# GpSimd adds the exponentials of pair 13 and of five second halves; TensorE sums what is left in one round

## The chip, the core and the metric

The kernel runs on one core of one Trainium2 chip. The metric is the time of the program on the device in microseconds (us). Engines are named as in the profile: PE is TensorE, DVE is VectorE, ACT is ScalarE, POOL is GpSimd, and SP only issues transfers here.

## The reference

The reference is attention, a soft mixture of experts and a two-layer MLP, all in float32 with the MLP's weights in float64:

```
scores = rope(q) @ rope(k).T / 8           # 4 x 8 heads, 576 positions, 64 wide
attn   = exp(scores - rowmax); attn /= sum(attn) + 1e-9
x      = attn @ v                          # becomes 2304 tokens x 512
x      = softmoe(x, phi, w1, w2)           # 8 experts, 32 slots
out    = relu(x @ w_in)**2 @ w_out
```

The change touches only the division: how the sum of a row's exponentials is formed.

## The kernel before

The 32 heads are worked in 16 pairs, numbered 0 to 15, two heads side by side on 128 partitions. Keys stand on partitions and queries along the columns. The 576 queries of a pair are two halves of 288 (h0 and h1). The 576 keys are four full units of 128 (u0 to u3) for each half, and one unit BOTH that holds the last 64 keys of both halves, so a pair has nine score units.

For one pair the work runs like this. SP loads the transposed q and k, plain and swapped (`load`). POOL applies the rotation in six operations, three each for k (t = 0) and q (t = 1) (`rope_pair`, recorded at L543). ACT rounds the result to a high part (`parts_pair`, L577), and POOL subtracts it to get a low part (L543 too). PE forms one set of products of high parts (`max_unit`, L654), and DVE reduces them to a stand-in for the maximum of each row (L665). PE transposes these maxima (`max_rows`, L684), and SP writes them back into SBUF as a row by a DMA (L703). Then `st_unit` forms the scores of a unit on PE from three products of high and low parts (L738) and subtracts the maximum with one more (L745); ACT takes the exponential (L758) into a buffer P. `pv_unit` multiplies it with V on PE (L789, and L784 for BOTH). `norm` sums the exponentials (L813), inverts on DVE and scales, and `logits` multiplies the finished rows with phi (L863, L868) and transposes them for the experts (L886).

The sum has two parts. POOL adds the first two units of a half into `acc` (L766). PE then multiplies `acc`, the other units and BOTH with a column of ones, 32 columns of the array for each, so that four such matmuls stand side by side; a round is two things by two heads. With four things (`acc`, u2, u3, BOTH) there are two rounds. For the pairs in `LATE`, 14 and 15, POOL adds u2 and u3 to `acc` too (L771), but not u3 of pair 15's second half; there the sum has two things and one round, and that last half has three things, whose second round uses two of the four places.

The order of all this is written out by hand. The table `Plan.ORDER` holds, for each kind of operation and engine, a rank for each operation in the order in which the program creates them; `retime` makes the rank its due time, and `emit` places operations in each engine's queue, the most urgent ready one first, by a table of costs. Engines then run their queues in that order and wait on semaphores. PE's operations have modes (r for scores and maxima, c and b for V, q for sums and logits, f for transposes), since they divide the array in different ways. The raw q and k of a pair lie in one of two buffers, so the load of pair p is issued when the low parts of pair p - 2 are done. Buffers P of the late pairs, and the buffers of raw data, parts and V, are given over to expert weights (`free`, L1174) as soon as their last readers are done.

After the attention come the slots and the experts (from about 295 us), fed by weights that SP loads, and the MLP (from about 335 us, L1806).

Of the kernel before, what the change touches and what calls it, by code (L numbers as in the profile page):

```python
# [38 lines left out]
class Plan:  # L39
# [29 lines left out]
            17, 19, 55, 79, 117, 150, 194, 224, 273, 305, 346, 361, 429, 454, 526, 531, 631, 633, 721, 724, 815, 818, 910, 914, 1013, 1015, 1101, 1104, 1193,  # L69
            1196, 1261, 1268  # L70
        ),
        ("parts_pair", "POOL", None): (
            22, 28, 60, 86, 124, 160, 199, 230, 279, 314, 359, 369, 435, 460, 532, 543, 637, 648, 732, 742, 825, 836, 922, 929, 1023, 1032, 1112, 1120, 1202,
            1210, 1273, 1281
# [6 lines left out]
        ),  # L81
        ("load", "SP", None): (
            36, 99, 173, 176, 180, 237, 240, 242, 322, 323, 327, 373, 377, 379, 468, 471, 473, 557, 561, 565, 659, 662, 665, 753, 755, 758, 846, 849, 852, 942,
            946, 949, 1043, 1045, 1047, 1131, 1133, 1136
        ),
        ("windows", "ACT", None): (
            23, 30, 82, 81, 156, 132, 226, 217, 309, 296, 406, 408, 499, 502, 606, 608, 698, 701, 791, 794, 884, 887, 988, 990, 1078, 1081, 1168, 1171, 1265,
            1275, 1331, 1332
# [24 lines left out]
        ("max_rows", "SP", None): (  # L113
            51, 62, 134, 136, 219, 222, 312, 317, 415, 417, 509, 510, 615, 618, 707, 710, 800, 803, 893, 896, 997, 1000, 1087, 1090, 1177, 1180, 1270, 1274, 1358,
            1355, 1422, 1418
# [11 lines left out]
            5, 6, 7, 8, 9, 10, 80, 83, 89, 91, 95, 101, 146, 148, 152, 155, 166, 170, 249, 252, 255, 266, 270, 275, 363, 453, 552, 655, 747, 841, 935, 1036, 1125,  # L127
            1214, 1302, 1368
# [1843 lines left out]
```

## Time and profile before

| | us |
|---|---|
| median of 3 runs | 566.4 (566.14 to 568.69) |
| the profiled execution | 565.09 |
| its span | 563.3 |
| PE busy | 544.0 (97%) |
| DVE busy | 398.6 (71%) |
| ACT busy | 295.7 (52%) |
| POOL busy | 229.9 (41%) |

The share is an average over stages: POOL does nearly all of its work in the first 285 us, and the DMA engines most of theirs between 265 and 340 us. The strip of 40 slices on the profile's page shows this; one slice is 14.1 us. The granted clock of PE is 1.00 in every stretch.

### The profile page before, as it was taken

How to read it: one execution, taken by the hardware profiler on the slowest of the kernel's cores; microseconds unless marked ns; L12 is line 12 of the kernel's file. 1: busy time of each engine (PE TensorE's matmuls, PEld its weight loads, DVE VectorE, ACT ScalarE, POOL GpSimd, SP SyncE). 2: the span in 40 equal slices, each digit the busy share in tenths (PEclk: the TensorE clock that was granted, in tenths of full speed). 3: DMA queues.
4: the chain of work that ended last, by engine and by line, in shares of the span. 5: the costliest groups of instructions: out<-in, count | busy, mean ns of one | idle time of the engine just before them, and what ended most of it. 6: DMA issues, size and time to landing. Idle time of an engine off the chain costs nothing.

```text
span 563.3 us, 13271 instructions
## 1 busy us (share of the span) xinstructions
PE 544.0 (97%) x5406; PEld 416.7 (74%) x5406; DVE 398.6 (71%) x878; ACT 295.7 (52%) x568; POOL 229.9 (41%) x178
## 2 busy tenths in 40 slices
PE   4999999999999999999999999999999999999996
PEld 3656666566665666666642258999999999999996
DVE  6587788888897887876468748965775595554553
ACT  2334545664555655544426548975944564354440
POOL 4999999988889788723610000000000000000000
PEclk9999999999999999999999999999999999999999
DMA  7447796877784357222989997132200220000333
GB/s 237 139 132 184 167 249 188 221 192 195 210 219 117 93 144 201 100 99 101 338 295 396 409 401 255 39 111 76 76 1 1 76 76 2 1 1 1 113 113 112
DMA packets 37741, 85.68 MB, mean 152 GB/s; under 512 B 12176, under 2 KB 12848, under 8 KB 36528
## 3 DMA queue, kind: packets, MB, share of 16 engines
q1 hardware_dynamic: 37398, 84.24, 48.3%
q8 instruction: 42, 0.69, 0.5%
q10 hardware_dynamic: 282, 0.59, 0.4%
q14 instruction: 19, 0.16, 0.1%
HBM read 77.92 MB, written 6.82 MB: 150 GB/s over the span
## 4 chain that ended last, share of the span: by engine, by line
PE 81%; DMA 9%; DVE 5%; POOL 2%; ACT 1%; issue 1%; SPq 0%; DVEq 0%
PE bank L1806 35%; PE bank L738 11%; PE obank L789 11%; PE bank L654 5%; PE bank L813 5%; PE bank L745 3%; PE obank L1736 3%; DVE mcol L665 2%; DMA w__1345<-in_w_dram 2%; DMA tEb<-in_w_dram 2%; DMA tLb<-in_w_in_dram 2%; PE obank L784 2%; PE bank L886 2%; DMA ident<-in_ident_dram 1%; POOL arena L543 1%; DMA w__448<-in_w_dram 1%
## 5 line engine op out<-in xcount | busy, mean ns | idle before, releaser
L758 ACT ACTIVATE tO<-bank 128x576 f32<-128x576 f32 x140 | 84.2, 650 | 84.4 <-PE bank L745 83.3
L665 DVE TENSOR_REDUCE mcol<-bank 128x2 f32<-128x576 f32 x144 | 103.2, 749 | 22.6 <-PE bank L654 13.1
L543 POOL TENSOR_TENSOR arena<-arena 128x576 f32<-128x576 f32 x78 | 111.0, 1444 | 8.8 <-DMA arena<-in_qk_dram 8.0
L1806 PE MATMUL bank<-w,tEb 128*128 128x256 f32 x864 | 106.5, 279 | 0.1
L1806 PEld LDWEIGHTS bank<-w,tEb 128*128 128x128 f32 x864 | 103.5, 188 | 2.4 <-issue 1.6
L789 PE MATMUL obank<-tO,pb 128*64 128x288 f32 x496 | 74.8, 419 | 0.0
L766 POOL TENSOR_TENSOR pb<-tO 128x576 f32<-128x576 f32 x30 | 42.9, 1430 | 31.0 <-ACT tO L758 29.4
L1806 PE MATMUL bank<-w,tEa 128*128 128x256 f32 x432 | 53.0, 278 | 0.0
L1806 PEld LDWEIGHTS bank<-w,tEa 128*128 128x128 f32 x432 | 51.6, 188 | 1.2 <-issue 1.2
L1806 PE MATMUL bank<-w,tO 128*128 128x256 f32 x432 | 51.6, 277 | 0.0
L1806 PEld LDWEIGHTS bank<-w,tO 128*128 128x128 f32 x432 | 51.1, 188 | 0.0
L789 PEld LDWEIGHTS obank<-tO,pb 128*64 128x64 f32 x496 | 29.8, 136 | 22.7 <-issue 9.3
L1747 ACT ACTIVATE pb<-obank 128x384 f32<-128x384 f32 x47 | 21.7, 495 | 36.8 <-PE obank L1736 36.8
L1747 ACT ACTIVATE w__1091<-obank 128x384 f32<-128x384 f32 x48 | 21.8, 491 | 36.5 <-PE obank L1736 36.2
L654 PEld LDWEIGHTS bank<-tEb 64*128 64x128 f32 x180 | 16.3, 184 | 21.5 <-DVE mcol L665 4.4
L813 PE MATMUL bank<-tO,ones 128*32 128x288 f32 x224 | 31.9, 409 | 0.0
L654 PE MATMUL bank<-tEb 64*128 64x288 f32 x180 | 30.5, 355 | 0.7 <-DVE mcol L665 0.5
L819 DVE STREAM_TRANSPOSE bank<-bank 128x288 f32<-128x288 f32 x32 | 15.9, 496 | 19.2 <-PE bank L813 15.8
L543 POOL TENSOR_TENSOR tLb<-arena,tEb 128x576 fp32r<-128x576 f32 x20 | 28.6, 1448 | 1.3 <-ACT tEb L577 1.3
L738 PE MATMUL bank<-tEb 64*128 64x288 f32 x180 | 28.5, 313 | 0.3 <-DVE mcol L665 0.2
L1736 PE MATMUL obank<-x,tO 128*128 128x384 f32 x95 | 26.8, 336 | 0.5 <-DVE tO L1664 0.5
L738 PE MATMUL bank<-tLb,tEb 64*128 64x288 f32 x180 | 26.6, 292 | 0.0
(299 smaller groups left out, 1095.2 us busy)
## 6 DMA issues: line engine op xcount, KB each, us to landing
arena<-in_qk_dram SPq DMA_DIRECT2D x14, 576.0 KB
arena<-in_qk_dram SPq DMA_DIRECT2D x12, 512.0 KB
arena<-in_w_dram SPq DMA_DIRECT2D x8, 512.0 KB
pb<-in_v_dram SPq DMA_DIRECT2D x12, 320.0 KB
arena<-in_qk_dram SPq DMA_DIRECT2D x3, 1152.0 KB
tLb<-in_w_in_dram SPq DMA_DIRECT2D x3, 1024.0 KB
pb<-in_w_in_dram SPq DMA_DIRECT2D x3, 1024.0 KB
w__448<-in_w_dram SPq DMA_DIRECT2D x4, 512.0 KB
```

What stands on the lines that cost most here:

```text
L543: ENG[e].tensor_tensor(out=o, in0=x, in1=y, op=how)
L654: nc.tensor.matmul(on_ring(tok)[:, j, 0:HQ], lhsT=x[rows], rhs=hi[rows, 0, HALF[c]], start=(u < BOTH or c == 0), stop=(u < BOTH or c == 1),)
L665: lambda e: nc.vector.tensor_reduce(out=mcol[:, h, :, u], in_=on_ring(tok)[:, :, 0:HQ], op=ALU.max, axis=AX.X),
L738: nc.tensor.matmul(st[:, j, 0:HQ], lhsT=w[rows], rhs=q[y][rows, HALF[c]], start=(i == 0 and (u < BOTH or c == 0)), stop=False,)
L745: nc.tensor.matmul(st[:, j, 0:HQ], lhsT=pick[rows, w : w + 128], rhs=mrow[rows, HALF[c]], start=False, stop=(u < BOTH or c == 1),)
L758: lambda e: nc.scalar.activation(out=pr, in_=on_ring(tok)[:, :, 0:HQ], func=AF.Exp, scale=0.125),
L766: lambda e: nc.gpsimd.tensor_tensor(out=acc, in0=one, in1=pr, op=ALU.add),
L789: nc.tensor.matmul(BANKS[6 + h][o, 0:HQ], lhsT=vr[:, u, j, :], rhs=pr[:, j, :], start=(h == 0 and u == 0), stop=(h == 1 and u == 3))
L813: nc.tensor.matmul(sm[QUAD[2 * j + w], 0:HQ], lhsT=one, rhs=x[:, j, :], start=(i == 0), stop=(i + w + 2 > last))
L1736: lambda e, i=i, t0=t0: nc.tensor.matmul(BANKS[i][:, 0:384], lhsT=wst_of()[:, 128 * fc : 128 * fc + 128], rhs=cst_of()[:, t0 : t0 + 384], ...
L1747: lambda e, i=i, h=h: nc.scalar.activation(out=rg_of()[:, 0, h], in_=BANKS[i][:, 0:384], func=AF.Relu),
L1806: nc.tensor.matmul(BANKS[c][:, cols], lhsT=gt[:, x, 128 * c : 128 * c + 128], rhs=wo[:, fc % 2, y, cols], start=(fc % FQ == 0 and i == 0 a ...
```

## The change

`folded` now reads a table. POOL adds u2 and u3 to `acc` for the second halves of pairs 8 to 12 and for both halves of pair 13 too, besides pairs 14 and 15; that is 14 more operations at L771 (the first halves of pairs 8 to 12 stay as they were). PE's sum then has two things and one round there. In the last sum, with three things, the third is now split: its first 144 columns go to one place and its other 144 to the next, so that the second round uses all four places with half the columns. The cost that `emit` takes for a sum follows. The ranks from about pair 4 on are new for every kind of operation.

POOL's order by the new ranks, from the rope of pair 14 to pair 13's adds (rope t d is operation d of k or q; lo is a low part): rope 14 0 0, rope 14 0 1, add 10 h1 u2, lo 13 1, add 10 h1 u3, add 11 h0, lo 13 0, rope 14 0 2, rope 14 1 0, rope 14 1 1, add 11 h1, rope 14 1 2, add 11 h1 u2, rope 15 0 0, rope 15 0 1, add 11 h1 u3, rope 15 1 0, add 12 h0, rope 15 1 1, lo 14 0, rope 15 1 2, lo 14 1, rope 15 0 2, add 12 h1, lo 15 1, add 12 h1 u2, lo 15 0, add 12 h1 u3, add 13 h0 (three), add 13 h1 (three). Before: rope 14 0 0, rope 14 0 1, rope 14 1 0, lo 13 0, lo 13 1, add 11 h0, rope 14 (three), add 11 h1, rope 15 (three), lo 14 0, lo 14 1, add 12 h0, rope 15 (three), add 12 h1, lo 15 0, lo 15 1, add 13 h0, add 13 h1.

On PE the second sum of pair 12 no longer stands beside the first: between them are the first two max units of pair 15, four product units of pairs 12 and 13 and five score units of pair 13. The transpose of pair 15's maxima now follows the transposes of pair 13's `logits` instead of preceding them.

```diff
--- before
+++ after
...
         ("max_rows", "PE", "f"): (
-            46, 57, 127, 211, 302, 405, 498, 605, 697, 790, 883, 987, 1077, 1167, 1260, 1349, 1406
+            46, 57, 127, 211, 302, 405, 501, 604, 697, 791, 883, 991, 1081, 1173, 1268, 1357, 1424
         ),
...
         ("st_unit", "PE", "r"): (
             64, 61, 70, 67, 77, 121, 115, 119, 125, 154, 151, 187, 178, 197, 206, 200, 203, 209, 257, 251, 276, 261, 288, 307, 292, 303, 337, 348, 345, 362, 351,
-            386, 398, 389, 393, 422, 438, 434, 451, 442, 479, 491, 482, 486, 514, 534, 530, 555, 539, 586, 596, 588, 592, 621, 639, 636, 654, 643, 681, 691, 683,
-            687, 714, 730, 727, 746, 735, 771, 782, 774, 778, 807, 824, 821, 840, 829, 866, 877, 869, 873, 901, 920, 917, 937, 924, 968, 978, 970, 974, 1005,
-            1021, 1019, 1035, 1025, 1061, 1071, 1063, 1067, 1094, 1110, 1107, 1124, 1114, 1149, 1159, 1152, 1155, 1184, 1201, 1199, 1213, 1205, 1243, 1253, 1245,
-            1248, 1233, 1290, 1292, 1307, 1314, 1323, 1311, 1333, 1341, 1309, 1373, 1380, 1383, 1376, 1370, 1395, 1367, 1385, 1435, 1442, 1439, 1445, 1460, 1468,
-            1464, 1461, 1470, 1473
+            386, 398, 389, 393, 422, 442, 434, 453, 438, 480, 493, 484, 488, 515, 532, 538, 536, 541, 585, 592, 595, 588, 619, 639, 633, 656, 635, 680, 691, 687,
+            683, 713, 728, 731, 748, 735, 773, 780, 776, 783, 804, 820, 824, 838, 826, 864, 874, 867, 871, 900, 925, 919, 937, 923, 970, 974, 978, 984, 982, 1020,
+            1031, 1043, 1022, 1062, 1073, 1069, 1064, 1097, 1114, 1118, 1127, 1111, 1152, 1156, 1159, 1163, 1197, 1205, 1216, 1219, 1200, 1250, 1255, 1237, 1259,
+            1239, 1300, 1303, 1306, 1297, 1325, 1322, 1346, 1354, 1309, 1393, 1387, 1395, 1398, 1383, 1410, 1381, 1390, 1449, 1451, 1456, 1460, 1474, 1482, 1475,
+            1478, 1484, 1487
         ),
...
         ("st_unit", "POOL", None): (
-            104, 138, 179, 223, 272, 321, 371, 410, 452, 508, 553, 612, 656, 700, 751, 793, 844, 886, 940, 992, 1042, 1080, 1129, 1170, 1217, 1263, 1301, 1340,
-            1387, 1393, 1401, 1410, 1421, 1446, 1453, 1458, 1467, 1471, 1479
+            104, 138, 179, 223, 272, 321, 371, 410, 461, 508, 582, 606, 667, 700, 758, 790, 839, 885, 896, 939, 955, 986, 996, 1029, 1060, 1085, 1107, 1124, 1133,
+            1172, 1190, 1212, 1227, 1272, 1293, 1307, 1313, 1319, 1328, 1353, 1363, 1370, 1401, 1408, 1413, 1422, 1434, 1459, 1467, 1471, 1481, 1485, 1493
         ),
...
         ("pv_unit", "PE", "c"): (
             73, 88, 97, 105, 135, 139, 141, 142, 168, 172, 212, 216, 233, 235, 238, 245, 271, 281, 294, 300, 328, 331, 333, 356, 366, 376, 380, 383, 424, 428,
-            430, 448, 457, 469, 472, 475, 519, 523, 525, 545, 562, 578, 580, 582, 626, 629, 632, 649, 660, 672, 675, 677, 717, 720, 722, 741, 752, 763, 766, 768,
-            811, 814, 816, 834, 845, 858, 861, 863, 906, 909, 911, 928, 944, 960, 963, 965, 1008, 1012, 1014, 1029, 1039, 1053, 1055, 1057, 1098, 1100, 1102,
-            1119, 1130, 1141, 1144, 1146, 1188, 1192, 1194, 1208, 1218, 1225, 1235, 1239, 1286, 1289, 1295, 1299, 1300, 1303, 1318, 1327, 1344, 1361, 1363, 1365,
-            1389, 1392, 1398, 1402, 1428, 1430, 1433, 1449, 1452, 1455, 1457, 1481, 1490, 1493, 1495, 1497
+            430, 448, 458, 470, 472, 474, 521, 523, 527, 557, 545, 577, 579, 581, 625, 627, 645, 648, 658, 672, 674, 677, 718, 720, 723, 741, 752, 764, 767, 770,
+            809, 811, 815, 831, 842, 854, 857, 860, 906, 908, 916, 930, 946, 960, 964, 967, 1011, 1014, 1017, 1024, 1034, 1046, 1055, 1057, 1102, 1104, 1106,
+            1122, 1131, 1142, 1144, 1146, 1191, 1193, 1195, 1209, 1223, 1230, 1233, 1244, 1287, 1291, 1296, 1318, 1311, 1316, 1333, 1341, 1349, 1358, 1374, 1375,
+            1403, 1406, 1407, 1415, 1440, 1444, 1446, 1463, 1466, 1469, 1472, 1496, 1504, 1507, 1509, 1511
         ),
...
         ("norm", "PE", "q"): (
-            130, 145, 221, 284, 319, 370, 414, 461, 507, 571, 614, 664, 706, 756, 799, 850, 892, 954, 996, 1044, 1086, 1134, 1176, 1228, 1269, 1277, 1350, 1356,
-            1420, 1454, 1475, 1486
+            130, 145, 221, 284, 319, 370, 414, 462, 509, 567, 613, 663, 706, 755, 800, 845, 893, 954, 1001, 1038, 1091, 1136, 1183, 1235, 1276, 1314, 1364, 1378,
+            1435, 1468, 1489, 1500
         ),
...
@@ -720,9 +720,11 @@
         i = (8 * p + 4 * h + u) % NPR if u < BOTH else NPR + p % 2
         return prs[i], ("P", i)
 
+    FOLDED = {8: ((), (2, 3)), 9: ((), (2, 3)), 10: ((), (2, 3)), 11: ((), (2, 3)), 12: ((), (2, 3)), 13: ((2, 3), (2, 3)), NP - 2: ((2, 3), (2, 3)), NP - 1: ((2, 3), (2,))}
+
     def folded(p, h):
 
-        return () if p not in LATE else (2,) if (p, h) == (NP - 1, 1) else (2, 3)
+        return FOLDED.get(p, ((), ()))[h]
 
     def st_unit(p, h, u, s, g):
         hi, lo, mrow, (pr, pk) = his[p % NHI], los[p % NLO], mrows[p % 2], p_slot(p, h, u)
@@ -797,6 +799,7 @@
 
         n = (2 * p + h) % 2
         things = [(accs[n], ("acc", n)), *(p_slot(p, h, u) for u in (2, 3, BOTH) if u not in folded(p, h))]
+        both = p_slot(p, h, BOTH)[1]
         last = len(things) - 1
         if last < 3:
             things.insert(1, things.pop())
@@ -807,14 +810,15 @@
             sm = on_ring(tok)[:, 0]
             for i in range(0, len(things), 2):
                 for j in range(2):
-                    for w in range(min(2, len(things) - i)):
-                        x, _ = things[i + w]
-                        one = half_ones[:, h] if i + w == (3 if last == 3 else 1) else ones[:, 0:32]
+                    for w in range(2):
+                        x, k = things[min(i + w, last)]
+                        one = half_ones[:, h] if k == both else ones[:, 0:32]
+                        cols = slice(0, HQ) if i + 1 <= last else slice(0, HQ // 2) if w == 0 else slice(HQ // 2, HQ)
                         nc.tensor.matmul(
-                            sm[QUAD[2 * j + w], 0:HQ], lhsT=one, rhs=x[:, j, :], start=(i == 0), stop=(i + w + 2 > last)
+                            sm[QUAD[2 * j + w], cols], lhsT=one, rhs=x[:, j, cols], start=(i == 0), stop=(i + 2 > last)
                         )
 
-        op({"PE": 0.97 if last > 1 else 0.49}, sums, g + T["sums"], [k for _, k in things], [("sm", n)], take="ring", tok=tok, mode="q")
+        op({"PE": (0.49, 0.73, 0.97)[last - 1]}, sums, g + T["sums"], [k for _, k in things], [("sm", n)], take="ring", tok=tok, mode="q")
         op(
             {"DVE": 0.47}, lambda e: nc.vector.transpose(out=on_ring(tok)[:, 1, 0:HQ], in_=on_ring(tok)[:, 0, 0:HQ]),
             g, [], [("sm", n)],
```

## Rows read from the trace of the kernel before

**Rows 1.** The page: busy tenths of an engine in 40 slices of the span.

```profile
PE   4999999999999999999999999999999999999996
...
POOL 4999999988889788723610000000000000000000
```

**Rows 2.** Stretches: length; busy of five engines (instructions); clock; DMA share; GB/s.

```profile
153.30:237.00 83.70, 83.70 (x994) 54.81 (x986) 69.50 (x171) 48.13 (x95) 70.48 (x50) 1.00 0.56 149
202.32:218.47 16.15, 16.15 (x198) 10.75 (x195) 13.08 (x34) 9.53 (x20) 14.08 (x10) 1.00 0.61 151
270.00:285.00 15.00, 14.58 (x177) 9.60 (x173) 6.85 (x24) 5.90 (x10) 8.46 (x6) 1.00 0.98 361
285.00:290.00 5.00, 4.38 (x43) 2.44 (x40) 3.63 (x14) 1.55 (x5) 0.00 (x0) 1.00 0.56 174
290.00:295.00 5.00, 4.30 (x36) 2.49 (x40) 2.58 (x12) 1.63 (x9) 0.39 (x1) 1.00 0.99 347
```

**Rows 3.** Timeline of PE at one sum: start, length, line, tiles, count.

```profile
169.10 0.41 PE L813 MATMUL bank<-pb,ones 128*32 128x288 f32 x1
...
169.35 0.41 PE L813 MATMUL bank<-pb,ones 128*32 128x288 f32 x1
...
169.84 0.41 PE L813 MATMUL bank<-tO,half_ones 128*32 128x288 f32 x1
...
170.19 0.40 PE L654 MATMUL bank<-tEb 64*128 64x288 f32 x2
```

**Rows 4.** The chain that ended last: start, length, engine, tile, line, count.

```profile
226.85 0.13 PE bank L654 x2
226.98 0.64 PE obank L789 x4
...
228.96 1.11 PE bank L813 x16
...
237.30 1.94 PE bank L813 x32
239.24 0.33 PE bank L654 x2
239.57 1.12 PE obank L789 x8
...
266.44 0.55 PE bank L886 x5
...
283.44 1.12 PE bank L813 x12
```

**Rows 5.** Timeline of POOL: start, length, operation, count, wait before it and releaser.

```profile
186.28 1.41 POOL L543 TENSOR_TENSOR arena<-arena 128x576 f32<-128x576 f32 x1 [4.06 <-DMA arena<-in_qk_dram]
...
204.59 4.18 POOL L543 TENSOR_TENSOR arena<-arena 128x576 f32<-128x576 f32 x3 [0.73 <-DMA arena<-in_qk_dram]
...
220.52 4.16 POOL L543 TENSOR_TENSOR arena<-arena 128x576 f32<-128x576 f32 x3 [0.51 <-DMA arena<-in_qk_dram]
...
228.77 4.28 POOL L543 TENSOR_TENSOR arena<-arena 128x576 f32<-128x576 f32 x3
```

**Rows 6.** Timeline of SP's queue, and one row of PE.

```profile
176.41 1.83 SPq L535 DMA_DIRECT2D arena<-in_qk_dram  x3
...
211.72 3.03 SPq L535 DMA_DIRECT2D arena<-in_qk_dram  x3
...
266.70 1.66 SPq L1174 DMA_DIRECT2D tO<-in_w_dram  x2
268.45 1.42 SPq L703 DMA_DIRECT2D tEa<-mrow  x2
...
272.95 0.40 PE L745 MATMUL bank<-tEa,pick 64*128 64x288 f32 x2 [0.42 <-DMA tEa<-mrow]
...
286.92 0.80 SPq L1174 DMA_DIRECT2D tO<-in_w_dram  x2
```

**Rows 7.** One line of DVE: duration in ns min/median/max, first and last start.

```profile
L1225 DVE TENSOR_SCALAR w__1091<-w__1091 x8: 409/1118/1464, 94.0 to 208.5; 128x512 f32<-128x512 f32 x8
```

More of the change, by code (lines that the diff above doesn't have):

```diff
@@ L68 @@
         ("parts_pair", "ACT", None): (
-            17, 19, 55, 79, 117, 150, 194, 224, 273, 305, 346, 361, 429, 454, 526, 531, 631, 633, 721, 724, 815, 818, 910, 914, 1013, 1015, 1101, 1104, 1193,
-            1196, 1261, 1268
+            17, 19, 55, 79, 117, 150, 194, 224, 273, 305, 346, 361, 436, 463, 530, 528, 628, 632, 725, 719, 819, 810, 911, 940, 994, 999, 1112, 1105, 1210, 1218,
+            1273, 1269
         ),
         ("parts_pair", "POOL", None): (
-            22, 28, 60, 86, 124, 160, 199, 230, 279, 314, 359, 369, 435, 460, 532, 543, 637, 648, 732, 742, 825, 836, 922, 929, 1023, 1032, 1112, 1120, 1202,
-            1210, 1273, 1281
+            22, 28, 60, 86, 124, 160, 199, 230, 279, 314, 359, 369, 444, 469, 560, 533, 640, 650, 751, 732, 848, 821, 922, 950, 1006, 1037, 1141, 1116, 1240,
+            1256, 1299, 1283
         ),
@@ L77 @@
             35, 41, 49, 45, 54, 68, 76, 96, 110, 116, 131, 143, 149, 171, 186, 193, 207, 214, 236, 244, 262, 250, 285, 295, 290, 304, 330, 336, 341, 352, 381,
[3 rows of a table removed]
[3 rows of a table added]
         ),
         ("load", "SP", None): (
-            36, 99, 173, 176, 180, 237, 240, 242, 322, 323, 327, 373, 377, 379, 468, 471, 473, 557, 561, 565, 659, 662, 665, 753, 755, 758, 846, 849, 852, 942,
-            946, 949, 1043, 1045, 1047, 1131, 1133, 1136
+            36, 99, 173, 176, 180, 237, 240, 242, 322, 323, 327, 373, 377, 379, 476, 478, 481, 573, 568, 571, 664, 666, 660, 766, 762, 759, 856, 853, 859, 956,
+            959, 962, 1045, 1051, 1048, 1153, 1148, 1151
         ),
         ("windows", "ACT", None): (
-            23, 30, 82, 81, 156, 132, 226, 217, 309, 296, 406, 408, 499, 502, 606, 608, 698, 701, 791, 794, 884, 887, 988, 990, 1078, 1081, 1168, 1171, 1265,
-            1275, 1331, 1332
+            23, 30, 82, 81, 156, 132, 226, 217, 309, 296, 406, 408, 500, 503, 605, 608, 698, 701, 792, 794, 884, 887, 992, 1005, 1082, 1084, 1174, 1176, 1260,
+            1258, 1336, 1338
         ),
@@ L126 @@
         ("load_v", "SP", None): (
-            5, 6, 7, 8, 9, 10, 80, 83, 89, 91, 95, 101, 146, 148, 152, 155, 166, 170, 249, 252, 255, 266, 270, 275, 363, 453, 552, 655, 747, 841, 935, 1036, 1125,
-            1214, 1302, 1368
+            5, 6, 7, 8, 9, 10, 80, 83, 89, 91, 95, 101, 146, 148, 152, 155, 166, 170, 249, 252, 255, 266, 270, 275, 363, 455, 562, 654, 747, 837, 936, 1030, 1128,
+            1215, 1323, 1379
         ),
@@ L174 @@
+            1396, 1453, 1457, 1461, 1464, 1429, 1423, 1524, 1522, 1494, 1490, 1514, 1513, 1518, 1516
         ),
         ("logits", "PE", "q"): (
-            220, 318, 411, 504, 611, 704, 797, 890, 994, 1084, 1174, 1267, 1360, 1417, 1478, 1502
+            220, 318, 411, 505, 611, 704, 796, 889, 997, 1087, 1178, 1275, 1362, 1437, 1492, 1517
         ),
         ("logits", "DVE", None): (
-            225, 320, 416, 505, 616, 708, 801, 894, 998, 1088, 1178, 1272, 1364, 1423, 1483, 1506
+            225, 320, 416, 511, 615, 708, 801, 894, 1003, 1092, 1184, 1279, 1366, 1441, 1497, 1520
@@ L180 @@
         ),
         ("logits", "PE", "f"): (
-            247, 335, 407, 501, 607, 699, 792, 885, 989, 1079, 1169, 1262, 1347, 1407, 1488, 1504
+            247, 335, 407, 502, 607, 699, 793, 886, 993, 1083, 1175, 1270, 1367, 1419, 1502, 1519
         ),
         ("logits", "ACT", None): (
-            254, 258, 338, 342, 413, 418, 506, 511, 613, 617, 705, 711, 798, 804, 891, 897, 995, 999, 1085, 1091, 1175, 1181, 1271, 1278, 1351, 1354, 1415, 1419,
-            1492, 1494, 1509, 1517
+            254, 258, 338, 342, 413, 418, 507, 513, 612, 618, 705, 711, 798, 803, 891, 897, 1002, 1008, 1089, 1095, 1180, 1186, 1278, 1282, 1373, 1376, 1427,
@@ L187 @@
+            1432, 1506, 1508, 1523, 1527
         ),
         ("prepare", "SP", None): (
-            390, 517, 483, 604, 589, 669, 684, 789, 775, 855, 870, 986, 971, 1050, 1064, 1166
+            390, 465, 485, 602, 589, 669, 684, 757, 777, 882, 868, 966, 975, 1077, 1066, 1171
         ),
         ("prepare", "ACT", None): (
-            431, 436, 463, 549, 556, 570, 619, 624, 653, 728, 745, 757, 808, 822, 839, 932, 938, 953, 1002, 1006, 1034, 1108, 1123, 1135
+            429, 431, 452, 556, 551, 570, 621, 649, 655, 729, 715, 746, 836, 813, 847, 935, 918, 948, 1015, 1018, 1041, 1126, 1108, 1137
@@ L193 @@
         ),
         ("prepare", "DVE", None): (
-            462, 512, 568, 597, 646, 667, 738, 783, 832, 851, 951, 979, 1027, 1046, 1116, 1160
+            447, 460, 564, 596, 651, 665, 734, 754, 844, 876, 942, 952, 1039, 1072, 1134, 1165
         ),
         ("slots_in", "DVE", None): (
-            515, 554, 558, 573, 898, 936, 939, 955, 1276, 1408, 1413, 1432, 1507, 1520, 1523, 1528, 1529
+            514, 554, 558, 569, 898, 938, 941, 957, 1281, 1421, 1426, 1443, 1521, 1533, 1537, 1542, 1543
@@ L199 @@
         ),
         ("slots_in", "ACT", None): (
-            520, 528, 535, 902, 905, 913, 918, 1282, 1280, 1285, 1287, 1511, 1515, 1513, 1518
+            517, 518, 525, 903, 902, 910, 915, 1288, 1290, 1292, 1294, 1525, 1529, 1531, 1534
         ),
         ("slots_in", "PE", "f"): (
-            548, 550, 931, 933, 1404, 1405, 1516, 1519
+            550, 552, 933, 934, 1417, 1418, 1530, 1532
         ),
         ("slots_in", "PE", "q"): (
-            566, 569, 948, 952, 1424, 1426, 1522, 1527
+            561, 565, 949, 953, 1431, 1439, 1536, 1541
@@ L208 @@
         ),
         (None, "PE", None): {
-            0: 1512, 1: 1521
+            0: 1526, 1: 1535
         },
         (None, "DVE", None): {
-            0: 1514, 1: 1524, 2: 1526
+            0: 1528, 1: 1538, 2: 1540
         },
         (None, "ACT", None): {
-            0: 1525
+            0: 1539
         },
```

13 lines of the change are left out of this document (6 added, 7 removed), and 46 rows, old and new, of the table ORDER.

## The prediction

> **What bounds the kernel now.** I first read the page's strip of 40 slices [rows 1]: TensorE (PE) is busy 9 tenths or more in every slice between the first and the last; GpSimd (POOL) goes from 9 tenths to mostly 8 in the 9th to the 17th slice and has little to do from the 18th (239 us) on. Then the table by stretch [rows 2]: in the pair from 202.32 to 218.47 us PE is busy for all 16.15 us and POOL for 14.08; from 270 to 285 us PE still has 14.58 of 15.00; from 285 to 290 us the DMA engines drop to 0.56, and from 290 us on they stand at 0.99. So the attention is bound by PE; behind it comes a stretch bound by DMA, whose first transfers are issued at 286.92 us, when the last pair releases its buffers [rows 6], after the queues have run dry. I conclude that what the end of the attention gains or loses goes through to the end at full size. Third I read PE in detail around one softmax sum, fourth the chain of waits, last POOL's and SP's queues.
>
> **Sums on PE.** The sum of one half-pair is eight matmuls, recorded as 16, four side by side. The first of each sub-round start at 169.10, 169.35 and (last) 169.84 us [rows 3]: 0.74 / 3 = 0.245 us each, four of them, 0.98 us. The chain has 1.11 us for a whole one with its mode change [rows 4]. A sum of two things needs two sub-rounds, and so gives back 0.49 us. Seven sums change (second halves of pairs 8 to 12, both of pair 13): 7 x 0.49 = 3.4 us. The very last sum, of three things, takes the same four sub-rounds today (x12, 1.12 us in rows 4, against 1.11 for x16); with its third thing split over half the columns each, two sub-rounds become half as long: 0.24 us. Together -3.6 us, all on the path, since PE is the bound there and the last sum stands in the chain.
>
> **Mode changes on PE.** The new tables interleave PE's work differently. When PE's 532 ranks of all its tables are sorted and neighbours of unlike mode are counted (mode r for max and score units, c and b for the products with V, q for sums and logits, f for transposes), there are 215 changes before and 225 after: 3 more between ranks 900 and 1100, one fewer to 1300, and the rest behind that, where pairs 13 to 15 run. A max unit takes 0.13 us among its like and 0.33 behind a product with V [rows 4]: 0.20 for entering r. Product units take 0.64 us for four and 1.12 for eight: 0.12 a matmul and 0.16 for the change. The sum has 1.11 - 0.98 = 0.13. Ten changes at 0.13 to 0.20 are 1.3 to 2.0 us, 1.6 by their middle. They lie on the path for the same reason; below zero is excluded, as no order here makes a change give time back.
> By "TensorEngine Tiling (Array Packing)" of the Trainium skill, section Key Properties, a change of tiling mode drains the engine. The trace agrees, with 0.13 to 0.20 us a change; who leaves the rule out would have -3.6 us where I have -2.0.
>
> **The adds on POOL.** 14 adds come in. In the trace POOL works at 1.39 us an operation (4.18 for three [rows 5]): 19.5 us. Five lie behind the last operations that prepare pair 15 (one of pair 12, four of pair 13), where POOL has little else to do. Nine lie ahead of them: 12.5 us, and from 153.30 to 237.00 us POOL has 83.70 - 70.48 = 13.2 us free [rows 2]. That fits only if nearly every wait is filled, and the waits for q/k loads can't be: a pair's load is issued when the pair two ahead has its low parts done (at 211.72 for pair 15 [rows 6]), and its rope starts at 220.52 [rows 5], 8.8 us later.
> A walk along POOL's new order, from 204.59 us, where the rope of pair 14 starts behind its own load [rows 5]: from there to the end of pair 13's low parts stand 7 operations instead of 5 (two new adds of pair 10, one of pair 11, one rope operation fewer): 204.6 + 7 x 1.39 = 214.3, against 211.6 now. Pair 15's load lands 8.8 us later: 223.1. To the end of its last rope operation there are 10 operations: 237.0. The copy to the high part and the hand-overs take about 1 us, an estimate: 238.0. PE wants it for the first max unit of pair 15. That stands at 239.24 now, behind both sums of pair 12 (1.94 us); in the new order only the first of them, of full length, is ahead of it, so 0.83 us sooner (1.94 - 1.11 [rows 4]), and PE is 4 x 0.49 - 3 x 0.16 = 1.5 us ahead by then: 236.9. So PE waits 1.1 us. The second sum of pair 12 then needs the fifth POOL operation behind that rope, at 237.0 + 5 x 1.39 = 244.0. Between the two PE has two max units (0.46), four product units (1.6 + 0.64) and five score units of eight matmuls (four times a max unit each, 2.6): 5.3 with a mode change 5.5. It comes there at 243.5 and waits 0.7 us more with the hand-over, 1.8 in all. Where the walk starts up to 1 us sooner, because pair 12's low parts now come in another order, 0.8 is left. I take 1.0. The ends: nothing, if the load also lands a little sooner; 2.9, if it takes 9.9 us as the one issued at 176.41 us did, for which POOL waited 4.06 us until 186.28 [rows 5, 6].
> By "SBUF — State Buffer" of the Trainium skill, section Who interferes with whom, a VectorE operation in a two-port mode and a GpSimd operation shut each other out for a whole instruction. The trace agrees: one VectorE tensor_scalar of one shape takes from 0.41 to 1.46 us [rows 7], about one POOL operation between the ends. With POOL gapless the six such and similar operations still to come (conversion of weights) could each cost VectorE up to 1.05 us; it has about 3 us free in each pair [rows 2], so no term comes of it.
>
> **The row maxima of pair 15.** Their transpose moves behind the five transposes of the logits step (0.55 us [rows 4]), while the score units of pair 15, which need the result through a DMA, stay where they are. PE waits 0.42 us for that DMA today [rows 6], so up to 0.55 more. On the other side that DMA is issued at 268.45 us behind two loads of 0.83 us each on SP [rows 6], issued once POOL's last add has read the buffers that they fill; where that add comes earlier, the DMA does too, and today's wait of 0.4 us can go. I take +0.1.
>
> **Sum.** -3.6 + 1.6 + 1.0 + 0.1 = -0.9 us. The profiled execution took 565.09 us (span 563.3 and 1.8 around it); the median of the runs shown, 566.4, stands 1.3 above it. The profile would go to 564.2, the median to 565.5.
>
> **Rivals.** (a) POOL keeps up and nothing waits: -3.6 + 1.6 = -2.0, 564.4. For it: today's last rope operation of pair 15 ends at 233.05 [rows 5], 6 us before PE's first use of the pair, so some lateness is covered; against: the walk above uses all of it. (b) Mode changes cost nothing because PE waits for PSUM at those points anyway: -3.6, 562.8. Against it: the 0.33 us max unit appears in the chain as work. (c) POOL becomes the bound of pairs 10 to 13: 12 operations a pair are 16.7 us, and with 0.6 us of load wait 17.3, against 16.15 of PE. It loses 1.1 us a pair, and every lost microsecond delays the next load. Over four pairs, with loads of 9.9 us for pairs 14 and 15 (2 us more), that is 6.4 us of wait, and -2.0 + 6.4 = +4.4: 570.8, slower. It decides from the point where the last rope operation of pair 15 ends after 242 us. Against it: POOL has 6 us in hand at pair 15 today. (d) The gain is lost behind the attention, because the loads issued from 270 us on fill the queues until about 286 us and the last four can't start sooner: 566.4. For it: 0.98 of DMA from 270 to 285; against: those loads are released by PE and POOL work that comes earlier too.
>
> **From this to the chances.** What a measurement can tell from no change is about 0.5%, 2.8 us: below 563.6 is faster, above 569.2 slower. My forecast 0.45, (a) 0.27, (b) 0.10, (c) 0.10, (d) 0.08. Faster: most of (b), a third of (a), a little of mine, 0.20. Slower: most of (c) and a little of the others, 0.10. The range: from (b) to a small form of (c), 562.7 to 568.0.
>
> **What would show it.** The seven sums with 8 records each and 0.49 us less; about ten more mode changes between 180 and 285 us; POOL without gaps from 190 to 247 us and the rope of pair 15 starting about 2 us later than 220.5; a wait of PE for ScalarE or POOL near 237 to 244 us, where today there is none. The forecast is wrong if that wait is over 3 us, if waits appear at the sums of pairs 9 to 11, or if the loads issued at 286.92 us today don't move with the end of the last pair.

## The result and the profile after

The changed kernel takes 572.21 us (median of four runs, 571.6 to 573.62) against 566.27 for the kernel before on the same chip: ratio 1.010, 95% interval 1.0066 to 1.0135, so 5.9 us slower. The prediction said 565.5, with a range of 562.7 to 568.0, and gave "slower" one chance in ten. The profiled execution took 571.6 us (span 569.8), 6.5 more than that of before.

Where the 6.5 us arise is read from four rows that both traces have, with the same work ahead of each: the third and the eleventh transpose of row maxima (L684), the last transposes of `logits` (L886, now L890), and the first matmul behind the experts' gate (L1652, now L1656). Timeline of PE, start and length first; the kernel before:

```profile
33.99 0.27 PE L684 MATMUL bank<-ident,m 128*10 128x128 f32 x1
...
167.95 0.28 PE L684 MATMUL bank<-ident,m 128*10 128x128 f32 x1
...
288.40 0.77 PE L886 MATMUL bank<-ident,pb 128*128 128x128 f32 x5
...
330.05 0.58 PE L1652 MATMUL obank<-arena,sit 128*32 128x128 f32 x8
```

and the changed kernel:

```profile
34.67 0.28 PE L684 MATMUL bank<-ident,m 128*10 128x128 f32 x1
...
174.05 0.28 PE L684 MATMUL bank<-ident,m 128*10 128x128 f32 x1
...
293.62 0.76 PE L890 MATMUL bank<-ident,pb 128*128 128x128 f32 x5
...
336.40 0.58 PE L1656 MATMUL obank<-arena,sit 128*32 128x128 f32 x8
```

What counts is by how much the distance between two rows grew. Up to the first row +0.68: the instructions there are the same, and the page's strip shows a lower granted clock in the second slice (below); other kernels with the same beginning started between 1.4 us earlier and 0.8 later than before, so this is chance. **From 34 to 168 us +5.42**, ahead of every new add, whose first stands at 175.67 us. **From there to the end of the attention -0.88**: this is the stretch that the prediction worked out, and its sum was -0.9. That the two agree so closely is luck: in the nine kernels below that have the new order there, this stretch measures from -2.10 to +0.83. **To the end of the gate +1.13.**

The page's strip of the changed kernel, which answers to [rows 1]: POOL has 9 tenths in the 14th to 17th slice and 8 in the 18th (7 to 8, and 2, before); PE falls to 8 in the second slice, where the granted clock is 6 tenths, in the 12th (157 to 171 us) and in the 24th (328 to 342 us, behind the gate).

```profile
PE   3899999999989999999999989999999999999996
...
POOL 4899999887888999984620000000000000000000
PEclk9699999999999999999999999999999999999999
```

The 8 in the 12th slice is all that the strip shows of the 5.4 us. From 34 to 174 us the waits of TensorE that show a releaser come to 4.1 us, nine of 0.2 to 1.6 us; in the kernel before they come to 0.9. What the other 2 us or so are made of was not traced. The waits are seen in the timelines. First what VectorE, ScalarE, GpSimd and TensorE do at 91 to 98 us (in brackets the idle time ahead and its releaser):

```profile
92.15 1.42 DVE L1229 TENSOR_SCALAR w__1088<-w__1088 128x512 f32<-128x512 f32 x1
93.60 1.43 DVE L665 TENSOR_REDUCE mcol<-bank 128x2 f32<-128x576 f32 x2
94.94 1.83 DVE L1241 SCALAR_TENSOR_TENSOR w__1088<-w__1088 128x512 int32<-128x512 int32 x1
96.69 0.75 DVE L665 TENSOR_REDUCE mcol<-bank 128x2 f32<-128x576 f32 x1
...
93.60 0.79 ACT L1236 ACTIVATE w__1088<-w__1088 128x512 f16<-128x512 f32 x1 [0.20 <-DVE w__1088 L1229]
94.37 0.65 ACT L760 ACTIVATE tO<-bank 128x576 f32<-128x576 f32 x1
...
91.87 1.41 POOL L543 TENSOR_TENSOR tLa<-arena,tEa 128x576 fp32r<-128x576 f32 x1 [0.22 <-ACT tEa L577]
93.23 1.61 POOL L543 TENSOR_TENSOR arena<-arena 128x576 f32<-128x576 f32 x1
94.80 1.42 POOL L768 TENSOR_TENSOR pb<-tO 128x576 f32<-128x576 f32 x1
96.17 1.86 POOL L543 TENSOR_TENSOR tLa<-arena,tEa 128x576 fp32r<-128x576 f32 x1
...
97.49 0.40 PE L654 MATMUL bank<-tEb 64*128 64x288 f32 x2 [0.61 <-DVE mcol L665]
```

VectorE's conversion of MLP weights (L1229, L1241) comes to its turn 0.3 and 0.14 us behind the start of a GpSimd operation, and ends 0.3 to 0.55 us behind that operation's end; the GpSimd operation behind it takes 1.61 and 1.86 us instead of 1.41. The ScalarE step L1236 waits for L1229, and an exponential (L760) stands behind it in the queue; behind L1241 stand the reductions of row maxima (L665), and TensorE waits for one. At 131 and 135 us TensorE waits for `mcol` again behind L1229 of 1.47 and L1241 of 1.93 us.

Second, ScalarE at 161 us, and TensorE behind it:

```profile
161.92 0.78 ACT L1224 ACTIVATE w__1088<-w__996 128x512 uint16<-128x512 uint16 x1 [2.28 <-DMA w__996<-in_w_out_dram]
162.56 0.62 ACT L760 ACTIVATE tO<-bank 128x576 f32<-128x576 f32 x1
...
163.24 0.40 PE L740 MATMUL bank<-tEb 64*128 64x288 f32 x2 [1.55 <-ACT tO L760]
```

A conversion waits 2.28 us for its own load, the exponential behind it waits too, and so does TensorE.

### The profile page after: what moved, and what is told of

It reads as the page before. It is cut to its first block, busy times and chain, and to the rows that moved or that the text cites. A ratio compares the mean times of both kernels' runs of the same rounds, so it can differ in the third digit from the quotient of the medians.

```text
span 569.8 us, 13198 instructions
## 1 busy us (share of the span) xinstructions
PE 545.8 (96%) x5354; PEld 415.1 (73%) x5354; DVE 402.4 (71%) x878; ACT 295.8 (52%) x568; POOL 249.9 (44%) x192
## 4 chain that ended last, share of the span: by engine, by line
PE 77%; DMA 11%; DVE 7%; issue 2%; ACT 1%; SPq 1%; DVEq 0%; ACTq 0%
PE bank L1810 35%; PE bank L740 11%; PE obank L791 10%; PE bank L654 5%; PE bank L817 4%; DVE mcol L665 4%; PE bank L747 3%; PE obank L1740 3%; DMA w__1365<-in_w_dram 2%; DMA tEb<-in_w_dram 2%; DMA w__996<-in_w_out_dram 2%; DMA tLb<-in_w_in_dram 2%; PE obank L786 2%; DMA ident<-in_ident_dram 1%; PE bank L890 1%
## 5 line engine op out<-in xcount | busy, mean ns | idle before, releaser
L760 ACT ACTIVATE tO<-bank 128x576 f32<-128x576 f32 x140 | 84.6, 650 | 87.0 <-PE bank L747 74.4
L665 DVE TENSOR_REDUCE mcol<-bank 128x2 f32<-128x576 f32 x144 | 103.6, 749 | 26.2 <-ACT tO L760 12.8
L791 PE MATMUL obank<-tO,pb 128*64 128x288 f32 x496 | 76.3, 422 | 0.0
L773 POOL TENSOR_TENSOR pb<-pb,tO 128x576 f32<-128x576 f32 x20 | 28.6, 1428 | 5.5 <-ACT tO L760 4.8
```

What stands on the lines that cost most here:

```text
L665: lambda e: nc.vector.tensor_reduce(out=mcol[:, h, :, u], in_=on_ring(tok)[:, :, 0:HQ], op=ALU.max, axis=AX.X),
L760: lambda e: nc.scalar.activation(out=pr, in_=on_ring(tok)[:, :, 0:HQ], func=AF.Exp, scale=0.125),
L773: op({"POOL": 1.39}, lambda e: nc.gpsimd.tensor_tensor(out=acc, in0=acc, in1=pr, op=ALU.add), g + 0.6, [pk], [ak])
L791: nc.tensor.matmul(BANKS[6 + h][o, 0:HQ], lhsT=vr[:, u, j, :], rhs=pr[:, j, :], start=(h == 0 and u == 0), stop=(h == 1 and u == 3))
```

## The experiments

Each run is compared with the kernel before on the same chip. The table gives the median, the ratio with its interval, and, from the same four rows of each trace, by how much the stretches 34 to 168 us (A), 168 to 288 us (B) and 288 to 330 us (C) are longer than in the kernel before. In e4 to e12 the planner is held to the ranks strictly in this part, so that each queue stands as its ranks say. A, B and C come from one execution of each kernel. Among the kernels whose first half has the old order, A lies between 0 and 2.3 us (e1, e4, e12 and e15), so a difference of A under about 2.3 us says nothing by itself; the medians are the safer measure. The profiled execution of e10 had a granted clock of 0.88 from 199.4 to 213.6 us (1.00 before), so its B is not compared.

| kernel | us | ratio | A | B | C |
|---|---|---|---|---|---|
| the change | 572.21 | 1.010 (1.0066 to 1.0135) | +5.42 | -0.88 | +1.13 |
| e1 old order up to 168 us | 567.02 | 1.001 (0.9993 to 1.0027) | +0.61 | -0.46 | +3.16 |
| e2 new order up to 168 us, no fold | 570.63 | 1.0068 (1.0044 to 1.0092) | +6.00 | +0.01 | +0.31 |
| e3 conversions put back | 569.60 | 1.0051 (1.0034 to 1.0067) | +4.16 | -0.56 | +3.03 |
| e4 folds in the old order | 578.36 | 1.020 (1.0173 to 1.0227) | +0.70 | +11.50 | +2.17 |
| e5 conversions later | 572.16 | 1.0111 (1.0088 to 1.0133) | +4.73 | +0.79 | +1.16 |
| e6 change, no VectorE conversion | 567.15 | 1.0008 (0.9983 to 1.0033) | +1.03 | -0.69 | +2.17 |
| e7 before, no VectorE conversion | 564.86 | 0.9979 (0.9963 to 0.9995) | -0.61 | -0.53 | +0.56 |
| e8 = e6 and e5 | 566.58 | 1.0012 (0.9997 to 1.0027) | +1.13 | -2.10 | +2.30 |
| e9 conversions in GpSimd's gaps | 570.59 | 1.0077 (1.0063 to 1.0091) | +3.65 | -0.33 | +1.31 |
| e10 without L1229 | 569.16 | 1.0059 (1.0032 to 1.0085) | +3.74 | +0.83 | +1.92 |
| e11 without L1241 | 567.93 | 1.0034 (1.0021 to 1.0047) | +1.40 | -1.15 | +0.91 |
| e12 pair 13 and split, old order | 565.10 | 0.9989 (0.9979 to 0.9999) | +1.81 | -1.17 | +0.27 |

**Which half of the order costs (e1, e2).** Up to rank 883 both tables issue the same set of operations, so they can be cut there.

```diff
 # e1, on the change: all ranks below 884 as before; e2, on the kernel before: all ranks below 884 as changed
-("prepare", "DVE", None): (447, 460, 564, 596, 651, 665, 734, 754, 844, 876, 942, ...
+("prepare", "DVE", None): (462, 512, 568, 597, 646, 667, 738, 783, 832, 851, 942, ...
...
```

> The whole change, but everything that the planner issues before the row maxima of pair 9 (ranks below 884, up to about 168 us) is put back in the order of the kernel before; the folds, the split of the last sum and the new order of what follows stay. Theory A (the new places of work in pairs 4 to 8, ahead of the first new add, cost about 5.4 us, and what follows gives back 0.9): 565.4 us, 0.9 below the kernel before. Rival B (GpSimd's new adds and their waits are what costs, and the early shift is a chance of that run): 570.5 us or more. Rival C (both halves of the order cost): about 568.

> The kernel before with none of the folds and with its own order from the row maxima of pair 9 on; only what is issued ahead of that (ranks below 884) stands in the new order. Nothing is added, only places are changed. Theory A: 571.7 us (5.4 more than before). Rival B: 566.3, no difference. Rival C: about 568.5.

The new order of pairs 4 to 8 is the cause of A: alone, with nothing added, it makes the kernel before 0.68% slower, with A at +6.0, and where it is undone A is back at +0.6. In e2 stretch A goes from the first to the second of these rows, in the kernel before from 33.99 to 167.95:

```profile
33.73 0.28 PE L673 MATMUL bank<-ident,m 128*10 128x128 f32 x1
...
173.71 0.28 PE L673 MATMUL bank<-ident,m 128*10 128x128 f32 x1
```

The other half of theory A, that what follows gives back 0.9 us, did not come out: e1's 567.02 us lies between A's 565.4 and C's 568. It gains 0.46 us in stretch B, loses more in C, and gains nothing in time.

**The folds without the order (e4).**

```diff
 # the change, with the ranks of the kernel before; the 14 adds go in at 896, 939, 996, 1029, ... less those ahead
 ("st_unit", "POOL", None): (..., 844, 886,
+896, 939, 942, 994, 996, 1029, 1046, 1084, 1107, 1124, 1135, ...
```

> All 14 new adds and the split of the last sum, but the order of the kernel before throughout; the adds are put between its operations at about the ranks that they have in the change. So 7 x 0.49 + 0.24 = 3.7 us less on TensorE, no added mode change. Theory A (the folds are good, the order is what costs): 562.7 us if GpSimd keeps up, up to 565 where sums wait for it. Rival B (the adds make GpSimd late in pairs 9 to 13): 568 or more, with waits of TensorE on GpSimd at the sums.

Rival B's time came, and more: 578.36 us, with GpSimd's adds making the sums wait. TensorE's matmuls of the sums (L806 in this kernel) wait for them six times, 9.4 us in all, as here:

```profile
199.39 0.69 PE L806 MATMUL bank<-pb,ones 128*32 128x288 f32 x1 [2.73 <-POOL pb L762]
...
237.23 0.69 PE L806 MATMUL bank<-pb,ones 128*32 128x288 f32 x1 [2.05 <-POOL pb L762]
```

So the new order of the later pairs is what makes the folds bearable, and the damage to the earlier pairs came with it.

**The place of the conversions (e3, e5).**

```diff
 # e3: their places on each engine as before
+("prepare", "DVE", None): (463, 511, 568, 601, 648, 667, 737, 783, 834, 850, ...
 # e5: tiles 1, 4 and 5 later by 20 ranks
+("prepare", "DVE", None): (464, 479, 564, 596, 651, 665, 752, 773, 863, 895, ...
```

> The whole change, but the weight conversion of the first six tiles (15 ScalarE, 10 VectorE operations and 11 DMA issues with ranks below 884) is put back to the place that it has in the kernel before on each of these engines, counted in operations ahead of it; everything else in its new order. Theory A1 (conversions that stand ahead of exponentials and wait for their own load or for GpSimd cause the early stalls): 567 us. Rival A2 (the new order of the score units, maxima and GpSimd's rope operations itself causes them): 571 to 572, as the change.

> The change, but the weight conversions of tiles 1, 4 and 5 (ScalarE, VectorE and the store; not the load) come 20 ranks, some 3.8 us, later; all else in the order of the change. Theory A1 (a ScalarE conversion that stands ahead of exponentials waits for its own load and holds them up): the stalls of TensorE at 160.7 us (1.9) and part of those at 90 to 97 us (1.9) go, 569 us. Rival A3 (VectorE's conversion operations, which GpSimd shuts out, hold up the row maxima): no change, 571.5 to 572.5.

Neither theory's number came out for e3: 569.60 us lies between them. It is 0.5% (2.8 us) better than the change, and A loses 1.3 of its 5.4 us. Between the transposes of row maxima from 85 us on, the change is longer than the kernel before by 1.9, -0.5, 1.4, 0.8 and 1.9 us, e3 by 0.5, 0.5, 0.5, 0.2 and 2.3: half of the loss of four pairs goes, that of the fifth stays. So the conversions' place in their own queues is not the whole cause. e5, at the time that A3 gave, speaks against A1: the stall at 161 us went, but its time came back elsewhere (the first VectorE conversion, now at 96.28 us, takes 1.25, and TensorE waits for `mcol` at 98.26 and 98.92 us).

**Without VectorE's conversion (e6, e7, e8, e10, e11).** The diff for all of them; e10 drops the first, e11 the second:

```diff
-op({"DVE": 0.4}, lambda e: nc.vector.tensor_scalar(out=z_of(), in0=z_of(), ..., op0=ALU.min, op1=ALU.max), ...)
-op({"DVE": 0.69}, lambda e: nc.vector.scalar_tensor_tensor(out=d_of().bitcast(I32), ..., op1=ALU.bitwise_or), ...)
```

> The change in its own order, but VectorE's two conversion operations of every tile are left out (16 operations; the converted weights are then not those of the reference). Theory A3: the stalls of TensorE behind them (93 to 97 us 1.3, 130 to 135 us 1.2, 146 to 150 us 0.8) go, 569 us. Theory A1: 572, since the waits for the loads stay.

> The kernel before, in its own order, with the same 16 VectorE operations left out: the reference for the run without them. Theories A1 and A3: 565.5 to 566.3, since TensorE has next to no stall behind them there. If the operations cost the kernel before as much as the change, A3 falls: then 563.

> Both edits on the change: conversions of tiles 1, 4 and 5 later by 20 ranks, and VectorE's 16 conversion operations left out. If A1 and A3 together are the whole cause: 566 to 567. Rival A2 (the order of score units, maxima and GpSimd's rope operations costs by itself): 569 or more, with stalls of TensorE left between 84 and 174 us.

> The change without VectorE's first conversion operation of each tile (tensor_scalar, for which ScalarE waits 5.5 us in four places); the second stays. If both weigh alike: 569.7. If the wait of ScalarE, with exponentials queued behind it, is the price: 567.5 to 568.5. If it is the second operation in front of the row maxima: 571.5.

> The change without VectorE's second conversion operation of each tile (scalar_tensor_tensor, up to 1.93 us, nobody but the store waits for its result); the first stays. If both weigh alike: 569.7. If its stand in front of the row maxima is the price: 567.5 to 568.5. If it is the first operation: 571.5.

This is the main answer. The same 16 operations cost the change 0.9% (1.010 to 1.0008) and the kernel before 0.2% (both e6 and e7 are faster than was expected of them, by 1.9 and 0.6 us), which leaves 0.7%, 4.0 us of the 5.9, to what the new order makes of them. Stretch A says nearly the same: 5.42 - 1.03 = 4.4 us in the change and 0.6 in the kernel before, so 3.8 of the 5.4 us. e6 ends its stretch A here (the change at 174.05):

```profile
33.99 0.28 PE L673 MATMUL bank<-ident,m 128*10 128x128 f32 x1
...
168.99 0.28 PE L673 MATMUL bank<-ident,m 128*10 128x128 f32 x1
```

What is left, 1.6 us between e6 and e7, is within what A differs by between executions, and by the medians (1.0008 and 0.9979) it is not clear of noise. Part of it may be ScalarE's conversions that wait for their loads with exponentials behind them; in e6:

```profile
138.73 0.79 ACT L1213 ACTIVATE w__1088<-w__996 128x512 uint16<-128x512 uint16 x1 [1.70 <-DMA w__996<-in_w_in_dram]
...
156.83 0.81 ACT L1213 ACTIVATE w__1088<-w__996 128x512 uint16<-128x512 uint16 x1 [1.05 <-DMA w__996<-in_w_out_dram]
```

In stretch A these waits for loads come to 4.6 us in e6 and 4.1 in the change, but TensorE's waits for exponentials to 0.9 and 2.2 us (0.2 in the kernel before): without VectorE's operations the late loads cost TensorE little. In e8 both waits are gone, at the time that A1 and A3 together gave (566 to 567), but e6 had nearly that time with them (567.15; 1.0008 against 1.0012). So no run shows that A1 costs anything.

The second VectorE operation, for whose result only a store waits, seems to weigh more than the first (0.66% against 0.41%, both 0.92%), and e11 has the time expected if its stand in front of the reductions is the price; but the intervals of e10 and e11 overlap. Since nothing that TensorE needs uses its result, it can only do harm through the queues: by standing in front of the reductions on VectorE, by what it does to GpSimd, or by when its store is issued. These were not told apart. In stretch B, e8 is 1.57 us shorter than e7, which would be near the -2.0 of rival (a); but e6, also without these operations, is only 0.16 us shorter, so this does not show it.

**Into GpSimd's gaps (e9).**

```diff
 # the change; VectorE's operations of tiles 1 to 4, the ScalarE step between them and the stores move
-("prepare", "DVE", None): (447, 460, 564, 596, 651, 665, 734, 754, 844, 876, ...
+("prepare", "DVE", None): (509, 589, 593, 677, 681, 774, 778, 797, 844, 876, ...
```

> The whole change, nothing left out; VectorE's eight conversion operations of tiles 1 to 4 (with the ScalarE step between them and the store) are moved to ranks at which the trace of the change shows GpSimd idle, waiting for a load (105.0, 119.2, 136.1, 153.7 and 157.0 us). Theory A3 (they cost because GpSimd shuts them out for the rest of its operation): they take 0.41 and 0.68 us instead of 1.4 to 1.9, and most of the 4.4 us of stall goes: 568.5 us. Rival A4 (VectorE or ScalarE is simply too full for them at any place): 571 to 572.

The time lies between the two theories, and the gain is not clear of noise: 0.2%, with overlapping intervals, and A 1.8 us shorter. Yet the operations became short. Six of the eight moved operations ran at their shortest, as here while GpSimd has nothing from 117.78 to 120.61 us:

```profile
117.88 0.65 DVE L1230 SCALAR_TENSOR_TENSOR w__1088<-w__1088 128x512 int32<-128x512 int32 x1
118.45 0.45 DVE L828 TENSOR_TENSOR pb<-obank,pb 128x288 f32<-128x288 f32 x1
118.82 0.41 DVE L1218 TENSOR_SCALAR w__1088<-w__1088 128x512 f32<-128x512 f32 x1
...
116.36 1.42 POOL L532 TENSOR_TENSOR arena<-arena 128x576 f32<-128x576 f32 x1
120.61 1.42 POOL L757 TENSOR_TENSOR pb<-tO 128x576 f32<-128x576 f32 x1 [2.83 <-ACT tO L749]
```

But stretch A keeps 3.65 us: two of the moved operations still ran longer (0.97 us at 102.92, 1.10 at 134.02, while GpSimd was at work), and the later stores made a wait of their own:

```profile
159.10 0.80 ACT L1213 ACTIVATE w__1088<-w__996 128x512 uint16<-128x512 uint16 x1 [1.21 <-DMA wi_single<-w__1088]
```

How long the conversions take does not go with A. Take the first ten of them, up to 174 us, and add up by how much each was longer than 0.41 or 0.68 us: 4.9 us in the kernel before, 6.3 in e1 (A +0.61), 5.8 in e3 (+4.16), 7.7 in the change (+5.42), 2.0 in e9 (+3.65). What is shown is that the new order and VectorE's conversions make the loss together; that it comes by GpSimd shutting them out, and not by their mere place between other work, is not shown, and e3 and e9 speak against it as the main way.

**The part of the change that is free (e12).**

```diff
-FOLDED = {8: ((), (2, 3)), 9: ((), (2, 3)), ..., 12: ((), (2, 3)), 13: ((2, 3), (2, 3)), ...}
+FOLDED = {13: ((2, 3), (2, 3)), ...}   # and the ranks of the kernel before, sums of pair 13 at 1354 and 1368
```

> The kernel before in its own order with only those parts of the change that fall where GpSimd has little to do: both sums of pair 13 in one round (four adds behind 247 us) and the split of the last sum; 2 x 0.49 + 0.24 = 1.2 us less on TensorE and no new interference in pairs 4 to 12. Theory: 565.0. Rival D (what the end of the attention gains is lost in the stretch bound by DMA): 566.0 to 566.8, no gain.

565.10 us, as expected, and B is -1.17. The interval (0.9979 to 0.9999) just leaves out no change: it is the fastest complete kernel here, by 0.1% over the kernel before and 1.1% over the change. Its stretch A, whose order is that of before, is 1.81 us longer in this one execution, and most of that (1.35 us) lies in one pair, in which VectorE's second conversion operation takes 1.74 us (at 162.88).

**The stretch bound by DMA (e13, e14, e15).** C is 0.9 to 3.2 us in the nine kernels with the new order of the later pairs, and 0 to 0.6 in the four with the old order and without folds in pairs 8 to 12. In e1 the DMA engines run dry at 296 us, and one issue of SP then takes 1.48 us (SP's queue):

```profile
296.05 0.33 SPq L1167 DMA_DIRECT2D w__448<-in_w_dram  x1
296.47 1.48 SPq L1167 DMA_DIRECT2D w__893<-in_w_dram  x1
298.05 0.38 SPq L1167 DMA_DIRECT2D w__448<-in_w_dram  x1
```

together with a packet of the instruction queue in that microsecond, and the DMA share of that stretch is 0.81, where the kernel before has 0.99 (the table by stretch, with the columns of [rows 2]; e1, then before):

```profile
295.00:300.00 5.00, 5.00 (x49) 1.54 (x52) 4.17 (x14) 1.63 (x5) 0.41 (x1) 1.00 0.81 246
```

```profile
295.00:300.00 5.00, 5.00 (x52) 1.56 (x48) 4.12 (x15) 1.91 (x5) 0.14 (x1) 1.00 0.99 372
```

In the kernel before, the long issue is one of the four of 3.15 us at 287.83, when nobody waits.

```diff
+pads = hbm.tile([n, 16], F32, name="pads")
+for i in range(n):  # 6, 8, 18
+    dma(lambda i=i: nc.sync.dma_start(out=pads[i : i + 1, :], in_=ident_in[0:1, 0:16]), ...)
```

> The first experiment's kernel (old order of the first half, the change from then on) with six tiny loads of 64 bytes issued on SyncE at about 260 us, where it waits 7 us anyway. Theory S (SyncE's instruction fetch falls on an issue that the dry DMA engines wait for): the slow issue at its 243rd instruction moves to about the 237th place of the old count, ahead of 291 us, where four loads are still queued; 1.5 us less, 565.5 us, and the DMA engines at over 0.9 from 295 to 300 us (0.81 before). Rival D2 (the stretch loses by the buffers' release or by chance): 567.0 as before, the lag stays.

> The change itself with eight such tiny loads at about 265 us. Theory S: the slow issue at 301.8 us moves ahead of 296 us, 1.0 us less, 571.2 us. Rival D2: 572.2.

> The kernel before with eighteen such tiny loads at about 260 us, so that the next fetch of SyncE (at about 303 us, its 267th instruction) comes at about the 249th, on one of the first loads behind the dry stretch at 296 us. Theory S: 1.0 to 1.5 us more, 567.2 us, with an issue of over 1 us between 296 and 300 us. Rival D2: 566.0, no change.

Measured: 567.62 us (1.0026, 0.9997 to 1.0055), 579.40 (1.0223, 1.0199 to 1.0246) and 582.67 (1.0292, 1.0275 to 1.0309). None has the time of theory S. It fell in the form that I gave it, and the test was a poor one. SP's queue in e14:

```profile
263.23 5.90 SPq L1911 DMA_DIRECT2D pads<-in_ident_dram  x8
271.98 0.81 SPq L1178 DMA_DIRECT2D tO<-in_w_dram  x2
272.89 1.50 SPq L703 DMA_DIRECT2D tEa<-mrow  x2
...
307.77 1.52 SPq L1178 DMA_DIRECT2D w__894<-in_w_dram  x1
```

With eight more issues ahead of it, the long issue moved by one: in the change it is the third load behind the dry stretch (301.84 us, 1.12 us), here the second. In e15 it did not move at all with eighteen: it is in the four loads at 306.91 us (3.14 us together), as in the kernel before. And a tiny load is no small thing: 5.90 / 8 = 0.74 us of SP each (16.03 / 18 = 0.89 in e15), so that the row maxima of pair 15 and the expert loads went out late. What sets the long issue, and what C loses by it, is open.

## Why the prediction was wrong

- **The step that failed** is where the sum starts. It begins at 153 us, and so puts the new order of pairs 4 to 8 at nothing, without a reason. It measured +5.42 us from 34 to 168 us, and +6.0 where nothing but that order was changed (e2). I had read that the ranks are new from pair 4 on, and counted mode changes in them (about 102 from 34 to 168 us in both traces, rightly no change), but not which operation stands in front of which.
- **The reasoning behind it** stands in the last sentence on the lock: VectorE "has about 3 us free in each pair, so no term comes of it". It was said of the six operations still to come, and in that stretch no loss shows. But it is wrong as an argument, and would have given nothing for pairs 4 to 8 as well, where the new order makes VectorE's conversions worth 4.0 us. Free time of an engine over a pair says nothing for an engine that works in order: the lateness falls on the reduction or the ScalarE step right behind, and TensorE is next (the rows at 91 to 98 us). The rule that I quoted there ("SBUF — State Buffer" of the Trainium skill, section Who interferes with whom) agrees with the trace: a tensor_scalar that takes 0.41 us alone took up to 1.51 us in the change, 1.10 more, for the 1.05 that I gave. Whether that lengthening, or the place in the queue, is what cost is open (e3, e9).
- **Sums**: right as far as tested. The seven have 8 records, the last one 16; e12, with three of these terms, shows -1.17 for 1.2, in one execution.
- **Mode changes**: the count is right. The trace has ten more behind 60 us, and nearly all of them lie behind 168 us. What they cost was not measured by itself.
- **POOL's lateness**: the walk is right, the wait is not. The rope of pair 15 starts at 229.68 us; the walk's 223.1 with the 6.1 us that PE was late by then is 229.2. Its last operation and the copy end at 243.5 and 244.2 us, where the walk with 6.1 has 243.1 and 244.1. But PE comes to the first max unit of pair 15 at 244.62, when the copy is done, and to the second sum of pair 12 at 250.41, as its last add ends. No wait for ScalarE or POOL shows at either, where I had 1.1 and 0.7 us:

```profile
242.06 1.42 POOL L543 TENSOR_TENSOR arena<-arena 128x576 f32<-128x576 f32 x1
243.51 0.69 ACT L577 ACTIVATE tEa<-arena 128x576 fp32r<-128x576 f32 x1 [0.52 <-POOL arena L543]
244.62 0.67 PE L654 MATMUL bank<-tEa 64*128 64x288 f32 x4
...
248.94 1.41 POOL L773 TENSOR_TENSOR pb<-pb,tO 128x576 f32<-128x576 f32 x1
250.41 0.43 PE L817 MATMUL bank<-pb,ones 128*32 128x288 f32 x1
```

  PE was 1.6 us less ahead than I had it (236.9 with 6.1 is 243.0). It had waited before, from 228 to 240 us, for about 1 us in all, and the one of these waits that shows a releaser is for the row maxima. So the term of 1.0 has about the size of a wait that arose elsewhere, which is luck:

```profile
230.46 0.40 PE L747 MATMUL bank<-tEb,pick 64*128 64x288 f32 x2 [0.50 <-DMA tEb<-mrow]
```

- **Rivals.** (c) has nearly the right time, 570.8, by the wrong way: in the pair from 210.20 to 226.30 us POOL is full, and PE's pair is 16.10 us all the same (16.15 in [rows 2]).

```profile
210.20:226.30 16.10, 16.10 (x198) 10.68 (x194) 13.22 (x34) 9.81 (x20) 16.10 (x12) 1.00 0.46 114
```

  (d) is true in part: the gain of stretch B is lost in C, in the profiled executions of the change and of e1. The loads at 286.92 us did move with the last pair, to 292.11; what came late was behind them.

## What to carry to other kernels

When a change brings a new order, read the order of every queue from the first rank that differs, and start the sum there. Look for operations that may take long (a shared port, a load of their own) in front of those for which the bound engine waits next; an engine's spare time does not cover them. Making such operations short is not enough by itself: in GpSimd's gaps they ran at their shortest, and the time hardly moved. And take from a rewritten schedule the part that stands alone first: pair 13 and the split, in the old order, gain 0.1%, where the whole change loses 1.0%.

## What the runs showed of the hardware

In the change, a VectorE operation of 0.41 us (tensor_scalar) or 0.68 us (scalar_tensor_tensor) on SBUF that met a running GpSimd operation of 1.4 us ended 0.3 and 0.55 us behind it (at 92.15 and 94.94 us). The same shapes took from 0.41 to 1.51 us and from 0.68 to 1.93 us, while VectorE's reductions out of PSUM kept their 0.72 to 0.76 us. The GpSimd operation that followed took 1.61 and 1.86 us. An issue of a 64-byte transfer from DRAM to DRAM took SP 0.7 to 0.9 us (e14, e15), more than most issues of 512 KB into SBUF behind the dry stretch (0.33 to 0.66 us in the kernel before).
